# Attention and routed experts on one core: the third pair's keys on three engines, GpSimd's work in pieces, one transpose later, two weight splits later

## The chip, the cores and the metric

The kernel runs on one core of a Trainium2 chip. The metric is the device time of one execution in microseconds (us). A core has five engines that run side by side, each through its own instructions in order: TensorE (PE in the profile, with its weight loads as PEld), VectorE (DVE), ScalarE (ACT), GpSimd (POOL) and SyncE (SP), which here only issues DMAs. A profile line such as L223 is line 223 of the kernel before the change.

## The reference

Two parts follow each other. Attention works on 4 batches of 8 heads with 768 positions of 64 elements. Every query sees a window of 31 keys around itself and 24 summaries of blocks of 32 keys (the maximum of the keys, the mean of the values):

```python
k_sum = k.reshape(B, H, nb, block, D).max(axis=3)
v_sum = v.reshape(B, H, nb, block, D).mean(axis=3)
mask_l = np.abs(pos[:, None] - pos[None, :]) < window
scores_l = scale * np.matmul(q, k.transpose(0, 1, 3, 2))
scores_s = scale * np.einsum('bhsd,bhnd->bhsn', q, k_sum) + np.log(block)
a = softmax(concatenate([where(mask_l, scores_l, -1e9), scores_s], axis=-1))
x = a @ concatenate([v, v_sum], axis=2)
```

The rows x (4 x 768 rows of 512) then go through eight experts of two layers, one expert per row:

```python
for s in range(S):
    fresh_e = int(np.argmax(logits[b, s]))
    if s == 0 or local_gate[b, s] < 0.5: e = fresh_e
    else: e = prev_e if prev_e >= 0 else fresh_e
    prev_e = e
    h = np.maximum(x[b, s] @ w1[e], 0.0)
    out[b, s] = p[e] * (h @ w2[e])
```

A row may keep its predecessor's expert, so the choice is a scan along each batch.

## The kernel before

**Attention** handles two heads at once, a pair; there are 16 pairs, four per batch. A pair is cut into two groups of 384 queries, so 32 steps `G` run, with three more to drain. In step G, PE makes the scores of group G (`s_mm`: the mask by a small matmul, L255, then queries times keys, L261), transposes the probabilities of group G-2 (`t_stage`, L282, copied out by ScalarE at L283) and multiplies group G-3 with the values (`a_mm`, L293). VectorE takes the maximum of the scores (`s_exp`, L268), ScalarE the exponentials (L272), and VectorE divides (`a_norm`, L304 to L306).

**The keys and values of a pair are laid out ahead**, while the pair before is worked on. Keys lie transposed in `kp`; `windows` (L220 on GpSimd, L218 on ScalarE) copies 12 overlapping windows of 96 keys into `kb`, scaled; `reduce_k` (L201, VectorE) takes the maxima of 32 keys; `summaries` (L223) writes them, repeated 12 times, behind each window. The scores of the pair need all of that. For the block means of the values, `fold_v` (L210, GpSimd) adds the two halves of each block, `reduce_v` (L205, VectorE) sums what is left, `sum_v` transposes the sums on PE (L227) and copies them out on ScalarE (L229), and `spread_v` (L232, GpSimd) writes them 12 times into the value tile `vw`, which `a_mm` reads. Two buffers serve `kp`, `kb` and the transposed values `vt`, three serve queries and `vw`.

**Order.** The program writes every engine's order out by hand. The loads of all these tiles and the writes of finished rows to `x_dram` (L311) stand in one queue, SP's; each waits there for its buffer and for the end of an earlier DMA, and whatever is behind it waits too. The first pair's keys are laid out before the loop by three engines, half of the windows on ScalarE and half on GpSimd, with the summaries on VectorE. From the second pair on GpSimd does, in this order, windows and fold in a pair's first step, and summaries and the spread of the current pair in its second. In step 0 SP also loads three tables (`wg`, `c32`, `cb16`, 337 KB) that the routing of the first batch needs from step 10 on.

**Routing** of a batch begins when its four pairs are done. `x_tile` makes the logits (L460 to L491) in steps 10 to 15, 18 to 23 and 26 to 31; `route` (steps 15, 23 and 31 on) is a chain of some thirty small VectorE steps and five small PE steps that finds each row's expert. They are slipped between attention's instructions by a planner: three calls `small` per step, with 3, 2 and 4 places; each step of the chain names its engine, and a step on PE may only be taken `AGE` = 2 calls after the one before it, so that PE does not stand for it. L522 is the first of them, the transpose of `val`, which L519 finishes. After the second batch, `early` picks rows of the most frequent expert (L702 to L721, on PE L715) and gathers them (L984), so that expert work can start with the last batch still in routing.

**Weights of the first expert** are fetched in 8 chunks of 1024 columns (`WFETCH` gives the steps) and split into a high and a low part (`WSPLIT`, `WBY`): ScalarE casts (L970), then VectorE subtracts in one instruction (L973) or GpSimd in four (L978). Chunks 0 to 3 are split in steps 24, 25, 27 and 29, by GpSimd, VectorE, GpSimd, VectorE; the others behind attention, at the places in `WLAST`. Four staging tiles serve all eight, so chunk 6 waits for the split of chunk 2, chunk 7 for that of chunk 3.

**The experts** follow, three matmuls per product (high x high, high x low, low x high), L1039 to L1041 and L1012 to L1014, until the end.

Of the kernel before, what the change touches and what calls it, by code (L numbers as in the profile page):

```python
# [9 lines left out]
F32 = mybir.dt.float32  # L10
# [9 lines left out]
P = 128  # L20
NP = H // 2
NW = S // 64
# [17 lines left out]

WFETCH = (21, 21, 22, 22, 26, 27, 29, 31)
WSPLIT = (24, 25, 27, 29)
WBY = "GVGVVGVG"

# [11 lines left out]

AGE = 2
C_T, C_PE, C_WAIT, C_LONG, C_DVE, C_LAT, AHEAD = 0.65, 0.8, 0.3, 0.9, 0.1, 0.05, 1.5
# [4 lines left out]
class Kernel:  # L63
# [81 lines left out]
    def attention(self, tick, last):  # L145
        nc, tc, ident = self.nc, self.tc, self.ident
        with ExitStack() as ctx:
# [59 lines left out]
            def fold_v(n):  # L207
                f = wk.tile([P, S // 2], F32, name="vf", bufs=1)
                v = by32(vts.pop(n))
                nc.gpsimd.tensor_tensor(out=by32(f, 16), in0=v[:, :, 0:16], in1=v[:, :, 16:32], op=ALU.add)  # L210
                folded[n] = by32(f, 16)

            def windows(n, eng=nc.gpsimd, t0=0, t1=NW):

                src = kp[n % 2][:, 64 * t0:64 * t0 + 1]
                win = bass.AP(src.tensor, src.offset, [src.ap[0], (64, t1 - t0), (1, WL)])
                if eng is nc.scalar:
                    eng.activation(out=kb[n % 2][:, t0:t1, 0:WL], in_=win, func=AF.Copy, scale=0.125)  # L218
                else:
                    eng.tensor_scalar(out=kb[n % 2][:, t0:t1, 0:WL], in0=win, scalar1=0.125, scalar2=1.0, op0=ALU.mult, op1=ALU.mult)  # L220
# [10 lines left out]
            def spread_v(n):  # L231
                nc.gpsimd.tensor_copy(out=vw[n % 3][WL:W, :, :, 0:D],  # L232
                                      in_=vss.pop(n).rearrange("p (h d) -> p h d", h=2).unsqueeze(1).to_broadcast([NB, NW, 2, D]))

# [87 lines left out]
            for G in range(last_g + LA):  # L322
# [7 lines left out]
                tick(G, 2)  # L330
                if GP < G < last_g and G % GP == 0:
                    sum_v(G // GP, self.spare[:, 1, 0:P])
# [7 lines left out]
                if G < last_g:  # L340
                    s_exp(G)
                    self.small(3, True)
                if G == 0:
                    for t, src in consts:
                        nc.sync.dma_start(out=t, in_=src)
                tick(G, 0)
                if G < last_g:
                    self.small(2, True)
                n, g = divmod(G, GP)
                if g == 1 and 0 < n < len(pairs) - 1:  # L350
                    reduce_v(n + 1, folded.pop(n + 1))
# [3 lines left out]
                if G < last_g:  # L355
                    n, g = groups[G]
                    N = len(pairs)
                    if g == 0:
# [4 lines left out]
                        elif n + 1 < N:  # L363
                            windows(n + 1)
                            fold_v(n + 1)
                            reduce_k(n + 1)
                        if n + 2 < N:
                            load_v(n + 2)
                        if 1 < n + 1 < N:
                            load_w(n + 1)  # L370
                    else:
                        if n + 1 < N and n:
                            summaries(n + 1)
# [33 lines left out]
    def small(self, n, pe=False):  # L407
# [3 lines left out]
        while self.credit > 0:  # L411
            heads = [h for h in list(self.steps)[:2] if h[0] != "PE" or pe and h[2] <= self.calls - AGE]
            if not heads:
                return
            head = min(heads, key=lambda h: h[0] == "PE")
            if len(heads) == 2 and head is self.last:
# [4 lines left out]
    def step(self, head):  # L421
        kind = head[0]
        self.last = head
        if kind == "PE":
            head[3] = max(self.t, head[3]) + C_PE
# [17 lines left out]
    def flow(self, dt):  # L443

        self.t += dt
        while True:
            heads = [h for h in self.steps[:2]
                     if (h[3] <= self.t if h[0] in ("PE", "WAIT") else max(h[3], self.q) <= self.t + AHEAD)]
            if not heads:
# [44 lines left out]
    def route(self, b):  # L494
# [24 lines left out]
        v.tensor_copy(out=val[0:1, 0:1], in_=sv[0:1, 0:1])  # L519
        yield "PE"  # L520
        m = self.bank("t")
# [846 lines left out]
```

## Time and profile before

| | |
|---|---|
| three runs | 479.96, 480.21, 481.28 us, median 480.21 |
| the profiled execution | 479.85 us, of which span from first to last instruction 478.1 |
| PE busy | 441.2 us (92%) |
| VectorE, ScalarE, GpSimd busy | 256.9, 216.3, 214.8 us |
| mean granted clock of TensorE | 0.976 |
| GpSimd's windows, fold, summaries, spread | 1.15, 1.01, 0.43, 1.46 us each |

A row of the order of time reads: start, duration, engine, line, operation, tile written <- tiles read, shapes, how many instructions were merged, and in brackets how long the engine had stood idle and what ended that. The table of stretches gives, for each engine, busy time and number of instructions, then the granted clock as a share, the mean busy share of the 16 DMA engines and GB/s.

### The profile page before, as it was taken

The numbers are of one execution on the slowest core, as the hardware profiler recorded it, in microseconds if no ns is written. First come the engines' busy times: TensorE is split into PE (matmuls) and PEld (weight loads), VectorE is DVE, ScalarE is ACT, GpSimd is POOL, SyncE is SP. The second block draws the span as 40 slices with busy tenths as digits, with TensorE's granted clock in tenths as the row PEclk, the third lists the DMA queues.
The fourth block names the chain that finished last, engine by engine and source line by source line (L and its number), as shares of the span: only waits on it lengthen the run. The fifth ranks groups of instructions, "written<-read, shape, count | busy, mean of one in ns | idle before, by whom it ended". The sixth has DMA issues, their size and how long they took to land. (4 is left out here: it accounts for less than half of the span.)

```text
span 478.1 us, 11984 instructions
## 1 busy us (share of the span) xinstructions
PE 441.2 (92%) x4400; PEld 383.0 (80%) x4400; DVE 256.9 (54%) x602; ACT 216.3 (45%) x479; POOL 214.8 (45%) x227
## 2 busy tenths in 40 slices
PE   6699989969889999999999999999999999999990
PEld 6477768757778789897989898989789898978970
DVE  5477597888874777993122222272745227274520
ACT  4588778878655222721211111272664127266400
POOL 2387454566502330852020202075887207588820
PEclk9799999999799999999999999999999999999995
DMA  8899969997530191392020202038389403938840
GB/s 301 316 378 334 384 238 344 360 374 288 193 125 15 29 387 71 86 352 73 23 67 23 67 24 67 22 108 334 121 330 330 149 23 97 345 119 309 290 178 27
DMA packets 23623, 92.05 MB, mean 193 GB/s; under 512 B 2927, under 2 KB 3567, under 8 KB 19440
## 3 DMA queue, kind: packets, MB, share of 16 engines
q1 hardware_dynamic: 18752, 76.11, 43.1%
q0 software_dynamic: 4640, 14.68, 9.3%
q8 instruction: 41, 0.67, 0.6%
q14 instruction: 46, 0.38, 0.3%
q10 hardware_dynamic: 144, 0.20, 0.1%
HBM read 78.40 MB, written 13.11 MB: 191 GB/s over the span
## 5 line engine op out<-in xcount | busy, mean ns | idle before, releaser
L1041 PE MATMUL bs<-xT,l 128*128 128x256 f32 x384 | 108.9, 284 | 1.2 <-DVE l L973 1.2
L1039 PE MATMUL bs<-xT,h 128*128 128x256 f32 x384 | 109.9, 286 | 0.0
L1040 PE MATMUL bs<-xT,h 128*128 128x256 f32 x384 | 108.8, 283 | 0.4 <-DVE xT L990 0.4
L984 POOL DMA_INDIRECT xg<-x_dram,gidx x32 | 37.1, 1160 | 124.8 <-POOLq L1215 54.2
L1045 ACT ACTIVATE hT<-bs 128x512 fp32r<-128x512 f32 x48 | 28.7, 598 | 121.6 <-PE bs L1041 121.1
L1047 DVE SCALAR_TENSOR_TENSOR hT<-bs,hT 128x512 fp32r<-128x512 f32 x48 | 33.1, 690 | 90.7 <-ACT hT L1045 79.7
L1012 PE MATMUL ba<-h,hT 128*128 128x512 f32 x192 | 77.8, 405 | 0.4
L1014 PE MATMUL ba<-h,hT 128*128 128x512 f32 x192 | 75.1, 391 | 0.0
L1013 PE MATMUL ba<-l,hT 128*128 128x512 f32 x192 | 75.0, 391 | 0.0
L978 POOL TENSOR_TENSOR l<-stg,h 128x256 fp32r<-128x256 f32 x84 | 73.9, 915 | 2.3 <-ACT h L970 1.6
L1041 PEld LDWEIGHTS bs<-xT,l 128*128 128x128 f32 x384 | 73.5, 191 | 1.8 <-DVE l L973 1.8
L1040 PEld LDWEIGHTS bs<-xT,h 128*128 128x128 f32 x384 | 73.5, 192 | 1.3 <-DVE xT L990 0.8
L1039 PEld LDWEIGHTS bs<-xT,h 128*128 128x128 f32 x384 | 73.5, 191 | 0.7 <-issue 0.2
L970 ACT CAST h<-stg 128x1024 fp32r<-128x1024 f32 x56 | 57.2, 1053 | 11.9 <-PE ba L1014 10.9
L272 ACT ACTIVATE pr<-bs,nm 128x120 f32<-128x120 f32 x192 | 51.9, 371 | 14.0 <-DVE nm L268 10.5
L973 DVE TENSOR_TENSOR l<-stg,h 128x1024 fp32r<-128x1024 f32 x35 | 46.5, 1338 | 16.2 <-ACT h L970 13.1
L1025 POOL DMA_INDIRECT out_dram<-yo,sidx x26 | 28.2, 1085 | 46.7 <-DVE yo L1024 21.3
L1012 PEld LDWEIGHTS ba<-h,hT 128*128 128x128 f32 x192 | 36.1, 188 | 8.0 <-issue 0.5
L1014 PEld LDWEIGHTS ba<-h,hT 128*128 128x128 f32 x192 | 36.0, 188 | 7.9
L1013 PEld LDWEIGHTS ba<-l,hT 128*128 128x128 f32 x192 | 36.2, 189 | 6.2
L261 PE MATMUL bs<-kb,q 64*64 64x120 f32 x768 | 27.2, 276 | 8.3 <-POOL kb L223 7.6
L268 DVE TENSOR_REDUCE nm<-bs 128x6 f32<-128x720 f32 x32 | 28.7, 898 | 5.9 <-ACT l L481 2.7
(236 smaller groups left out, 661.7 us busy)
## 6 DMA issues: line engine op xcount, KB each, us to landing
stg<-in_w SPq DMA_DIRECT2D x32, 1024.0 KB, 6.8
vw<-in_vW SPq DMA_DIRECT2D x16, 780.0 KB, 6.9
kp<-in_kT SPq DMA_DIRECT2D x16, 384.0 KB, 5.4
q<-in_qT SPq DMA_DIRECT2D x16, 384.0 KB, 6.8
vt<-in_vT SPq DMA_DIRECT2D x16, 384.0 KB, 6.7
x_dram<-xs SPq DMA_DIRECT2D x8, 768.0 KB, 4.6
wst<-in_w SPq DMA_DIRECT2D x8, 512.0 KB, 7.1
xg<-x_dram,gidx POOLq DMA_INDIRECT x32, 3.8
```

The costliest lines, as they stand in the source:

```text
L272: nc.scalar.activation(out=pr[:, h, u, :], in_=sp[:, h, u, :], func=AF.Exp, bias=nm[:, h, u:u + 1], scale=1.0)
L970: self.nc.scalar.copy(out=hi, in_=src)
L973: eng.tensor_tensor(out=lo, in0=src, in1=hi.bitcast(F32), op=ALU.subtract)
L978: eng.tensor_tensor(out=lo[:, p], in0=src[:, p], in1=hi[:, p].bitcast(F32), op=ALU.subtract)
L984: self.nc.gpsimd.indirect_dma_start(out=t, out_offset=None, in_=rows, in_offset=bass.IndirectOffsetOnAxis(ap=self.gidx[:, i:i + 1], axis=0))
L1012: nc.tensor.matmul(out=ps, lhsT=ah, rhs=wh, start=first, stop=False)
L1013: nc.tensor.matmul(out=ps, lhsT=ah, rhs=wl, start=False, stop=False)
L1014: nc.tensor.matmul(out=ps, lhsT=al, rhs=wh, start=False, stop=last)
L1039: nc.tensor.matmul(out=ps[:, j], lhsT=wh, rhs=xh, start=(k == 0), stop=False)
L1040: nc.tensor.matmul(out=ps[:, j], lhsT=wh, rhs=xl, start=False, stop=False)
L1041: nc.tensor.matmul(out=ps[:, j], lhsT=wl, rhs=xh, start=False, stop=(k == KT - 1))
L1047: nc.vector.scalar_tensor_tensor(out=l, in0=ps, scalar=0.0, in1=h.bitcast(F32), op0=ALU.max, op1=ALU.subtract)
```

## The change

1. **Third pair's keys.** In step 2 the windows are halved between ScalarE and GpSimd and VectorE writes the summaries, as for the first pair. There is no fold for the third pair; VectorE sums its values whole, in step 4 instead of 3, and the transpose of the sums goes to step 5. The three tables are loaded in step 4 instead of 0. From the fourth pair on, the fold is written behind the maxima instead of ahead of them; these are different engines.
2. **GpSimd in pieces.** Windows go in pieces of at most 4 windows (three for a pair, two for a half), folds in two pieces, spreads in four.
3. **Routing's first transpose.** For the first two batches L522 is marked "PE late": it may be taken 3 calls after the step before it instead of 2.
4. **Splits.** Chunk 0 is split by VectorE and chunk 1 by GpSimd (swapped); chunk 2 stays with GpSimd and chunk 3 with VectorE, but they move from steps 27 and 29 to 30 and 31. Chunks 6 and 7 are fetched in steps 31 and 32 instead of 29 and 31.

```diff
-WFETCH = (21, 21, 22, 22, 26, 27, 29, 31)
-WSPLIT = (24, 25, 27, 29)
-WBY = "GVGVVGVG"
+WFETCH = (21, 21, 22, 22, 26, 27, 31, 32)
+WSPLIT = (24, 25, 30, 31)
+WBY = "VGGVVGVG"
...
-AGE = 2
+ON_PE = {"PE": 2, "PE late": 3}
...
             def fold_v(n):
...
+                for i in range(0, NB, NB // 2):
+                    p = slice(i, i + NB // 2)
+                    nc.gpsimd.tensor_tensor(out=f[:, p], in0=v[:, p, 0:16], in1=v[:, p, 16:32], op=ALU.add)
...
             def windows(n, eng=nc.gpsimd, t0=0, t1=NW):
+                if eng is nc.gpsimd and t1 - t0 > NW // 3:
+                    for t in range(t0, t1, NW // 3):
+                        windows(n, eng, t, min(t + NW // 3, t1))
+                    return
...
             def spread_v(n):
...
+                for t in range(0, NW, NW // 4):
+                    nc.gpsimd.tensor_copy(out=vw[n % 3][WL:W, t:t + NW // 4, :, 0:D], in_=vs.to_broadcast([NB, NW // 4, 2, D]))
...
-                if GP < G < last_g and G % GP == 0:
+                if 2 * GP < G < last_g and G % GP == 0 or G == 2 * GP + 1:
                     sum_v(G // GP, self.spare[:, 1, 0:P])
...
-                if G == 0:
-                    for t, src in consts:
-                        nc.sync.dma_start(out=t, in_=src)
...
-                if g == 1 and 0 < n < len(pairs) - 1:
+                if g == 1 and 1 < n < len(pairs) - 1:
                     reduce_v(n + 1, folded.pop(n + 1))
...
-                            windows(n + 1)
-                            fold_v(n + 1)
-                            reduce_k(n + 1)
+                            if n > 1:
+                                windows(n + 1)
+                                reduce_k(n + 1)
+                                fold_v(n + 1)
+                            else:
+                                windows(2, nc.scalar, 0, NW // 2)
+                                windows(2, nc.gpsimd, NW // 2, NW)
+                                reduce_k(2)
+                                summaries(2, nc.vector)
+                        if n == 2:
+                            reduce_v(2)
                         if n + 2 < N:
                             load_v(n + 2)
                         if 1 < n + 1 < N:
                             load_w(n + 1)
+                        if n == 2:
+                            for t, src in consts:
+                                nc.sync.dma_start(out=t, in_=src)
                     else:
-                        if n + 1 < N and n:
+                        if n + 1 < N and n > 1:
                             summaries(n + 1)
...
         yield "DVE"
         v.tensor_copy(out=val[0:1, 0:1], in_=sv[0:1, 0:1])
-        yield "PE"
+        yield "PE late" if b < 2 else "PE"
         m = self.bank("t")
         nc.tensor.transpose(out=m[0:NU, 0:P], in_=val, identity=self.ident)
```

More of the change, by code (lines that the diff above doesn't have):

```diff
@@ L207, in fold_v @@
             def fold_v(n):
-                f = wk.tile([P, S // 2], F32, name="vf", bufs=1)
+                f = by32(wk.tile([P, S // 2], F32, name="vf", bufs=1), 16)
                 v = by32(vts.pop(n))
-                nc.gpsimd.tensor_tensor(out=by32(f, 16), in0=v[:, :, 0:16], in1=v[:, :, 16:32], op=ALU.add)
-                folded[n] = by32(f, 16)
+                for i in range(0, NB, NB // 2):
+                    p = slice(i, i + NB // 2)
+                    nc.gpsimd.tensor_tensor(out=f[:, p], in0=v[:, p, 0:16], in1=v[:, p, 16:32], op=ALU.add)
+                folded[n] = f
             def windows(n, eng=nc.gpsimd, t0=0, t1=NW):
+                if eng is nc.gpsimd and t1 - t0 > NW // 3:
+                    for t in range(t0, t1, NW // 3):
+                        windows(n, eng, t, min(t + NW // 3, t1))
+                    return
                 src = kp[n % 2][:, 64 * t0:64 * t0 + 1]
@@ L231, in spread_v @@
             def spread_v(n):
-                nc.gpsimd.tensor_copy(out=vw[n % 3][WL:W, :, :, 0:D],
-                                      in_=vss.pop(n).rearrange("p (h d) -> p h d", h=2).unsqueeze(1).to_broadcast([NB, NW, 2, D]))
+                vs = vss.pop(n).rearrange("p (h d) -> p h d", h=2).unsqueeze(1)
+                for t in range(0, NW, NW // 4):
+                    nc.gpsimd.tensor_copy(out=vw[n % 3][WL:W, t:t + NW // 4, :, 0:D], in_=vs.to_broadcast([NB, NW // 4, 2, D]))
             folded = {}
@@ L411, in small @@
         while self.credit > 0:
-            heads = [h for h in list(self.steps)[:2] if h[0] != "PE" or pe and h[2] <= self.calls - AGE]
+            heads = [h for h in list(self.steps)[:2] if h[0] not in ON_PE or pe and h[2] <= self.calls - ON_PE[h[0]]]
             if not heads:
                 return
-            head = min(heads, key=lambda h: h[0] == "PE")
+            head = min(heads, key=lambda h: h[0] in ON_PE)
             if len(heads) == 2 and head is self.last:
@@ L423, in step @@
         self.last = head
-        if kind == "PE":
+        if kind in ON_PE:
             head[3] = max(self.t, head[3]) + C_PE
@@ L447, in flow @@
             heads = [h for h in self.steps[:2]
-                     if (h[3] <= self.t if h[0] in ("PE", "WAIT") else max(h[3], self.q) <= self.t + AHEAD)]
+                     if (h[3] <= self.t if h[0] in ON_PE or h[0] == "WAIT" else max(h[3], self.q) <= self.t + AHEAD)]
             if not heads:
```

## The prediction

> **What bounds the kernel now.** I read the page first, for the span and the slices; then the waits of TensorE (PE); then the order of time around each wait.
>
> ```profile
> span 478.1 us, 11984 instructions
> ...
> PE   6699989969889999999999999999999999999990
> ```
>
> A slice is 12 us. From the slice at 143 us on, when the experts have begun, PE is at nine tenths or more until the last: nothing of the change lies there, and time won earlier should move that stage forward whole. Before that lies attention, and there PE has holes. Its waits from 60 to 124 us (engine, line, what it waited for: us in total, times, longest):
>
> ```profile
> PE bt L522 <- DVE val L519: 2.7, 2, 1.4
> PE bs L261 <- POOL kb L223: 2.4, 1, 2.4
> PE bs L227 <- DVE va L205: 1.7, 2, 0.9
> PE bt L715 <- DVE ebt L711: 1.2, 1, 1.2
> ```
>
> These are 8.0 us, and each row meets a part of the change. A longer one stands at the start, in order of time:
>
> ```profile
> 13.14 1.56 ACT L272 ACTIVATE pr<-bs,nm 128x120 f32<-128x120 f32 x6
> 13.37 1.46 POOL L232 COPY vw<-vs 24x1536 f32<-24x1536 f32 x1 [3.69 <-ACT vs L229]
> 13.52 0.95 DVE L201 TENSOR_REDUCE ks<-kp 128x24 f32<-128x768 f32 x1 [1.65 <-DMA kp<-in_kT]
> ...
> 15.93 0.35 PE L255 MATMUL bs<-me 64*64 64x360 bf16 x4
> 19.45 1.00 POOL L210 TENSOR_TENSOR vf<-vt 128x384 f32<-128x384 f32 x1 [3.38 <-DMA vt<-in_vT]
> 20.42 0.43 POOL L223 TENSOR_SCALAR kb<-ks 128x288 f32<-128x288 f32 x1
> ...
> 20.90 1.11 PE L261 MATMUL bs<-kb,q 64*64 64x120 f32 x24 [4.63 <-POOL kb L223]
> ```
>
> The third pair's keys landed at 13.5, where the maximum of L201 starts; but on GpSimd (POOL) the key summaries of L223 stand behind the fold of L210, which waits until 19.45 for values. PE stands from 16.28 to 20.90 for an instruction whose own data was there.
>
> **Part 1, the start.** In the new order nothing of the third pair's keys stands behind the values. ScalarE (ACT) lays out its half after the exponentials, from 14.70. VectorE (DVE) ends the maximum at 14.47 and then writes the summaries, which take GpSimd 0.43. GpSimd is the last, and there the short pieces count. These are the sizes that the trace has (ns: shortest, median, longest):
>
> ```profile
> L220 POOL TENSOR_SCALAR kb<-kp x16: 675/1152/1741, 4.9 to 118.8; 128x1152 f32<-128x1152 f32 x15, 128x576 f32<-128x576 f32 x1
> L210 POOL TENSOR_TENSOR vf<-vt x14: 1002/1012/1020, 19.4 to 119.9; 128x384 f32<-128x384 f32 x14
> L978 POOL TENSOR_TENSOR l<-wst,h x16: 722/732/1513, 101.3 to 160.9; 128x256 fp32r<-128x256 f32 x16
> ```
>
> Windows of 1152 elements take 1.152 and of 576 take 0.675: 0.83 ns an element and 0.20 us an instruction (with two inputs 1.012 for 384 and 0.732 for 256: 2.2 ns and 0.17). An added piece costs about 0.17, since neighbours overlap by some 0.03 (L223 starts at 20.42, L210 ends at 20.45). No row shows the spread, L232, in another size; I take the same 0.17 for it, between 0 and its whole 1.46, which it would be if its time went by the instruction. Six pieces are added per pair, 1.0 on top of 1.15 + 1.01 + 0.43 + 1.46 = 4.05, so 5.05. The Trainium skill, GPSIMD Engine Reference, section 2.1, puts the dispatch of an instruction at "tens of cycles"; as an estimate, 50 cycles of its 1.2 GHz are 0.04 us, so by the page six pieces would cost 0.25, and the 0.2 that I take off below would go. No row here shows it so cheap.
>
> GpSimd then ends the spread at 13.37 + 1.46 + 0.5 = 15.3 and its half of the windows, in two pieces, at 15.3 + 0.85 = 16.2. PE's mask matmul ends at 16.28, so the scores start at 16.3 and not at 20.9: 4.6 won. What is late next? The pitch of the steps after the stall, and the stretches around it (us, busy time of PE, PEld, DVE, ACT, POOL, granted clock, DMA share, GB/s):
>
> ```profile
> 28.50 0.85 PE L261 MATMUL bs<-kb,q 64*64 64x120 f32 x24 [0.57 <-POOL kb L223]
> ...
> 33.72 0.79 PE L261 MATMUL bs<-kb,q 64*64 64x120 f32 x24
> 20.00:22.00 2.00, 1.10 (x25) 0.80 (x26) 1.45 (x5) 0.00 (x0) 0.85 (x2) 0.84 0.21 43
> 22.00:30.00 8.00, 7.43 (x126) 6.12 (x125) 5.62 (x12) 5.65 (x20) 5.44 (x5) 0.83 1.03 394
> 30.00:40.00 10.00, 10.00 (x233) 8.41 (x232) 9.02 (x20) 9.04 (x31) 7.78 (x8) 1.00 0.99 363
> ```
>
> Two steps take 33.72 - 28.50 = 5.2, so 2.6 each. Three things stand behind the new start.
>
> VectorE sums the third pair's values itself now, unfolded: the 768 elements of L201, so about its 0.95. Ahead of that, from 16.0 on, stand two normalisations, the second pair's sum, a maximum of scores and one of keys, which I estimate at the same 0.95 each, with a pause of 0.4 for PE's attention matmuls: it ends near 22.0. The transpose of that sum (L227, now a step later) is due on PE near 20.2. That is a new wait of 1.8, and the step's probability transposes are queued behind it.
>
> GpSimd does the second pair's spread from 19.2 to 21.2, then windows 1.5, fold 1.2 and summaries 0.43: 24.3. The fourth pair's scores, at 28.50 now, can start then: 4.2 won. The 1.8 is paid from the half clock after the stall, which the trace has at 0.83 over 8 us (1.4 lost). From there GpSimd needs 5.05 a pair where PE needs 5.2: it keeps up, barely, and I take 0.2 off.
>
> DMA is full from 22 to 40. Only the hole at 20 to 22 can be filled (2.0 x 0.79 = 1.6). On SP's queue the fourth pair's values, which wait for the fold's end at 20.45 now, will wait for VectorE's sum of the second pair's, near 18, with the next windows of values, keys and queries queued behind; the three tables that move from the first step to the third pair's first step (337 KB, 0.9 us at 363 GB/s) only change places. So data comes 1.6 earlier while 4.2 are wanted, and the rest must be slack between landing and use. There is some, since from 24 to 124 us two of thirteen folds waited for data:
>
> ```profile
> POOL vf L210 <- DMA vt<-in_vT: 6.3, 2, 3.8
> ```
>
> I take **4.0**, from 1.6 (only the hole filled) to 6.0 (4.6 and all of the 1.4).
>
> **Part 2, routing.** Small VectorE steps of routing are long beside GpSimd and short without it:
>
> ```profile
> 62.08 1.46 POOL L232 COPY vw<-vs 24x1536 f32<-24x1536 f32 x1
> ...
> 62.53 1.07 DVE L506 TENSOR_TENSOR eq<-l_all,mx 128x48 f32<-128x48 f32 x1
> ...
> 134.67 0.20 DVE L506 TENSOR_TENSOR eq<-l_all,mx 128x48 f32<-128x48 f32 x1
> ```
>
> L506 ends at 63.60, just behind L232 at 63.54: VectorE waited out the whole GpSimd instruction. With pieces of 0.5 to 0.6 it waits for the rest of one, 0.3 on average, instead of 0.87: 0.5 saved, and as much for its sister L508 beside the fold, so 1.0 per batch. The late transpose takes L522 behind the next step's scores and probability transposes, so PE no longer stands there 1.4 each time. Its two followers move a call as well, but by the planner's credits (3, 2 and 4 a step) the matmuls of L555 fall on the same call as before, so nothing later moves. With PE free, VectorE's own chain is the limit, so I count its 1.0 for each of two batches: **2.0**, from 0.4 to 4.4 (L522 and L227 whole).
>
> **Part 3, the first two splits.**
>
> ```profile
> 101.32 2.78 POOL L978 TENSOR_TENSOR l<-wst,h 128x256 fp32r<-128x256 f32 x4 [4.18 <-ACT h L970]
> ...
> 104.50 1.23 DVE L973 TENSOR_TENSOR l<-wst,h 128x1024 fp32r<-128x1024 f32 x1 [1.51 <-ACT h L970]
> ```
>
> GpSimd's split of step 24 holds the summaries, and with them PE for the 2.4 of the waits. With the two swapped that goes, but VectorE's split now stands in step 24, ahead of step 25's maximum: 1.23 and a wait for ScalarE's cast that I put at 0.8, about half of the 1.51. Against it that later split leaves VectorE, mostly beside other work; I count 0.4. GpSimd's split a step later is covered by its pause before the next windows. 2.4 - 2.0 + 0.4 = **0.8**, from -1.2 (that cover gone, 2.0 lost) to 2.4.
>
> **Part 4, the two moved splits.**
>
> ```profile
> 115.25 3.58 POOL L978 TENSOR_TENSOR l<-wst,h 128x256 fp32r<-128x256 f32 x4 [2.13 <-issue]
> ...
> 134.56 0.89 ACT L283 COPY pt<-bt 120x384 f32<-120x384 f32 x2
> L970 ACT CAST h<-wst 128x1024 fp32r<-128x1024 f32 x6 | 6.5, 1086 | 0.0
> 123.00:131.00 8.00, 7.86 (x112) 6.43 (x112) 5.87 (x21) 5.20 (x16) 3.37 (x3) 0.57 0.41 115
> ```
>
> At 115 GpSimd's work moves up by 3.6, so the VectorE steps ahead of L715 meet less of it: I take 0.8 of that wait's 1.2. The VectorE split that leaves step 29 frees VectorE where PE is the bound (7.86 of 8.0 at a clock of 0.57): nothing. In steps 30 and 31 a cast of 1.1 comes ahead of the copies at 134.56, on which PE's last attention matmuls wait, and on GpSimd the last spread comes behind a split of 2.8; the two delays run side by side: -1.1. The last two fetches go a step or two later on SP and are used well into the expert stage: nothing. Together **-0.3**, from -3.0 (split and spread in the open) to 1.2.
>
> Sum: 4.0 + 2.0 + 0.8 - 0.3 = **6.5**. The profiled execution took 479.85 (its span and 1.75 around it); the median of the three runs is 480.21, 0.36 more. 479.85 - 6.5 = 473.35, and with the 0.36 **473.7**.
>
> **Rivals.** *The clock too.* In the row of 123 to 131 PE runs at 0.57, behind a wait of only 1.2. If that wait shrinks and the clock stays full, PE's work there takes 7.86 x 0.57 = 4.5, and VectorE's 5.87 becomes the limit: 2 more, and with part 2 nearer its upper end 469 to 471.5. Against it, where such a stretch falls may differ from run to run. The Trainium skill, TensorE: Matmul & The Clock Gate, Part 1, ties half clock to a whole window of about 3.4 us without work; by that rule the 1.2 was not the cause, the stretch stays, and this rival falls.
>
> *The start given back.* The transfers set the pace from 22 to 40, and part 1 brings its 1.6; the sum is 4.1, and with parts 2 and 3 a little short 476 to 478. For it stands the DMA share of 0.99 to 1.03.
>
> *Not what it says.* VectorE gets no turn between GpSimd's pieces and waits for all of them; part 2 is 0 and the time 475.7. Against it, the four pieces from 115.25 took 3.58 and those from 101.32 took 2.78, so something did get between.
>
> *Slower.* GpSimd becomes the bound of the three pairs from 24 to 40, because a piece costs more than 0.17. With six pieces of p each the loss is 3 x (4.05 + 6p - 5.2); it eats the 6.5 and 1.4 more from p = 0.63 on, and with p = 0.8 it is 10.9 and the time 484.6. Only the spread could cost so much; the other rows say 0.2.
>
> **How the numbers follow.** About 0.3% (1.4 us) can be told from no change. Forecast 0.50 (472 to 476), clock 0.25, start given back 0.12, not what it says 0.04, slower 0.05, every part at its lower end and no change 0.04. Faster 0.91, within 0.04, slower 0.05. The range takes in the clock's case from 469.0 and the start given back up to 478.0.
>
> **What would show it.** Right: no wait of PE for L223 between 16 and 21, and full clock there; a wait of about 1.8 at L227 near 20 to 22; the fourth pair's scores near 24.3; L506 and L508 under 0.6; no wait at L522; an expert stage of unchanged length. Wrong: windows, fold or spread clearly over 1.5, 1.2 and 2.0 in their pieces; GpSimd without a pause and PE waiting on it from 24 to 40; waits for DMA there; or a last attention matmul that waits for the last spread by more than 1.

## The result and the profile after

The changed kernel takes 473.49 us (median of 4 runs, 471.6 to 473.81) where the kernel before took 480.08 in the same comparison: a ratio of 0.984, 95% interval 0.982 to 0.986, so 6.6 us less by the medians and 7.6 by the ratio. (Differences in us given with a ratio below are taken from it.) The ratios leave out two executions far above their fellows, one of 551 us of the kernel before and one of 844 us of the kernel with the second transpose late. The profiled execution took 473.66, with a span of 471.8 instead of 478.1. Its code has moved down: L261 is now L270 (scores), L223 L231 (summaries), L227 L235 (transpose of the value sums), L232 L242 (spread), L506 and L508 L523 and L525, L522 L539, L525 L542 (the scan `pm`), L528 L545 (the second routing transpose), L973 L990 and L978 L995 (splits on VectorE and GpSimd), L293 L302, L990 L1007, L1040 L1057.

PE's waits after the change (line, what it waited for: us in total, times, longest) answer to the first list of the prediction:

```profile
PE bt L545 <- DVE pm L542: 4.1, 2, 3.1
PE bs L235 <- DVE va L206: 2.6, 3, 1.9
...
PE ba L302 <- POOL vw L242: 2.4, 1, 2.4
...
PE bs L270 <- POOL kb L231: 0.4, 1, 0.4
...
PE bt L732 <- DVE ebt L728: 0.2, 1, 0.2
```

The three waits that the change was aimed at are gone or small: 7.6 for the summaries became 0.4, 2.7 at L522 became nothing, 1.2 for `ebt` became 0.2. Of the 2.6 for the summed values, 1.9 are the new wait near the start and 0.7 what is left of the 1.7 in routing. But 4.1 stands for the scan, which no row of before had, and 2.4 for the last spread. The start in order of time:

```profile
14.23 0.67 ACT L226 ACTIVATE kb<-kp 128x576 f32<-128x576 f32 x1
...
14.95 0.85 PE L270 MATMUL bs<-kb,q 64*64 64x120 f32 x24
15.01 0.82 POOL L228 TENSOR_SCALAR kb<-kp 128x384 f32<-128x384 f32 x2
...
21.19 0.28 PE L235 MATMUL bs<-ident,va 128*24 128x128 f32 x1 [1.92 <-DVE va L206]
...
23.74 1.41 PE L270 MATMUL bs<-kb,q 64*64 64x120 f32 x24
```

The scores of the third pair start at 14.95 instead of 20.90, beside GpSimd's half of the windows. They need not wait for it: a step's matmuls read six windows (`t = 2 * (NG * g + u) + c`, with `NG` = 3), and the pair's first step reads windows 0 to 5, which are ScalarE's half. The new wait at L235 is 1.92, and the fourth pair's scores start at 23.74. The two small VectorE steps of routing each run four times, for the first two batches beside GpSimd. In the first batch L508 stood beside the fold (L506, 1.07 us beside the spread, is in the prediction):

```profile
64.74 1.02 POOL L210 TENSOR_TENSOR vf<-vt 128x384 f32<-128x384 f32 x1
...
64.87 0.95 DVE L508 TENSOR_TENSOR eq<-eq,c 128x48 f32<-128x48 f32 x1
```

In the changed kernel:

```profile
58.16 1.84 POOL L242 COPY vw<-vs 24x384 f32<-24x384 f32 x4
...
58.61 0.55 DVE L523 TENSOR_TENSOR eq<-l_all,mx 128x48 f32<-128x48 f32 x1
...
60.09 1.46 POOL L228 TENSOR_SCALAR kb<-kp 128x384 f32<-128x384 f32 x3
...
60.43 0.22 DVE L525 TENSOR_TENSOR eq<-eq,c 128x48 f32<-128x48 f32 x1
```

L523 gets between the pieces of the spread and takes 0.55 instead of 1.07. L525 is short for another reason: it comes earlier, GpSimd's spread takes longer, and so it no longer stands beside the fold but beside the windows, where it takes 0.22, hardly more than the 0.21 of the third batch with GpSimd idle. The second batch has the same pairs of numbers within 0.01. GpSimd's order from 31 to 38 shows what its pieces take, and that it now waits for data three times:

```profile
31.97 1.46 POOL L228 TENSOR_SCALAR kb<-kp 128x384 f32<-128x384 f32 x3 [0.53 <-DMA kp<-in_kT]
33.88 1.15 POOL L213 TENSOR_TENSOR vf<-vt 128x192 f32<-128x192 f32 x2 [0.46 <-DMA vt<-in_vT]
...
36.16 1.84 POOL L242 COPY vw<-vs 24x384 f32<-24x384 f32 x4 [0.73 <-DMA vw<-in_vW]
```

Where the time was won is read off the start of the scores of some steps, of the first second-layer matmul, and of the two ends, each subtracted from that of before (51.72, 93.87, 113.09, 161.28, 465.70 and 478.07). "Again" is another execution of the same kernel on another chip; the other rows are the experiments below. Negative is later than before.

| kernel | step 13 | step 24 | step 28 | second layer | last matmul | span |
|---|---|---|---|---|---|---|
| changed | 3.9 | 4.7 | 4.3 | 5.2 | 5.3 | 6.3 |
| changed, again | 4.3 | 5.1 | 5.3 | 6.2 | 6.1 | 7.1 |
| part 1 alone | 4.0 | 3.8 | 3.2 | 4.0 | 4.7 | 4.6 |
| pieces alone | -2.2 | -1.2 | -0.8 | 1.0 | 1.2 | 1.7 |
| late transpose alone | -0.8 | -1.5 | -4.8 | -4.9 | -4.6 | -4.8 |
| splits alone | -0.2 | -0.2 | -3.3 | -2.1 | -2.4 | -2.6 |
| without late | 3.7 | 4.6 | 4.9 | 4.4 | 5.1 | 6.0 |
| without the swap | 3.9 | 4.7 | 4.9 | 4.3 | 4.1 | 4.8 |
| last two splits back | 3.6 | 4.4 | 5.1 | 6.9 | 6.8 | 7.8 |
| second transpose late too | 4.0 | 5.4 | 6.4 | 4.9 | 4.7 | 5.7 |
| splits in 25, 26, 27, 29 | 4.0 | 4.8 | 4.3 | 3.2 | 3.4 | 4.3 |
| the same, second transpose late too | 3.4 | 4.8 | 6.2 | 5.9 | 6.3 | 7.2 |
| finer pieces | 0.4 | 1.7 | 2.6 | 3.6 | 4.0 | 4.4 |

Each row is one execution; two executions of one kernel differ by up to 1 here. The one execution of before that they are subtracted from took 479.85, while the medians of before on the other chips are 481.1 to 481.4, so the ratios give more than the last column, by 0.1 to 3.1 us. A verdict on time needs the ratio of several runs, which each experiment gives against the kernel before on its own chip (481.1 to 481.4 there).

### The profile page after: what moved, and what is told of

Same layout as the page of the kernel before. It is cut to its first block, busy times and chain, and to the rows that moved or that the text cites. A ratio compares the mean times of both kernels' runs of the same rounds, so it can differ in the third digit from the quotient of the medians.

```text
span 471.8 us, 12078 instructions
## 1 busy us (share of the span) xinstructions
PE 440.5 (93%) x4400; PEld 383.6 (81%) x4400; DVE 254.9 (54%) x603; ACT 216.5 (46%) x480; POOL 225.2 (48%) x316
## 5 line engine op out<-in xcount | busy, mean ns | idle before, releaser
L1057 PE MATMUL bs<-xT,h 128*128 128x256 f32 x384 | 108.8, 283 | 0.5 <-DVE xT L1007 0.5
L995 POOL TENSOR_TENSOR l<-stg,h 128x256 fp32r<-128x256 f32 x84 | 74.6, 921 | 2.5 <-ACT h L987 1.6
L1057 PEld LDWEIGHTS bs<-xT,h 128*128 128x128 f32 x384 | 73.5, 192 | 1.4 <-DVE xT L1007 1.0
L990 DVE TENSOR_TENSOR l<-stg,h 128x1024 fp32r<-128x1024 f32 x35 | 47.4, 1364 | 16.3 <-ACT h L987 13.1
L242 POOL COPY vw<-vs 24x384 f32<-24x384 f32 x64 | 30.7, 521 | 8.7 <-ACT vs L237 6.1
L302 PE MATMUL ba<-vw,pt 120*64 120x65 f32 x768 | 31.5, 235 | 2.9 <-POOL vw L242 2.4
```

The source lines that it names most:

```text
L990: eng.tensor_tensor(out=lo, in0=src, in1=hi.bitcast(F32), op=ALU.subtract)
L995: eng.tensor_tensor(out=lo[:, p], in0=src[:, p], in1=hi[:, p].bitcast(F32), op=ALU.subtract)
L1057: nc.tensor.matmul(out=ps[:, j], lhsT=wh, rhs=xl, start=False, stop=False)
```

## The experiments

The theory after the result: the start is won by part 1, the pieces pay in routing, and the late transpose and the splits only exchange waits, because VectorE has little time to spare from step 24 on. The rivals: every part brings its own share, as the prediction summed it; or the data sets the pace and the start is partly given back.

**Part 1 alone** (label p1_start), on the kernel before:

```diff
+                                windows(2, nc.scalar, 0, NW // 2)
+                                windows(2, nc.gpsimd, NW // 2, NW)
+                                reduce_k(2)
+                                summaries(2, nc.vector)
...
+                        if n == 2:
+                            reduce_v(2)
```

with the later transpose of these sums, the later tables and the order of the fold that belong to it.

> The kernel before with part 1 alone: the third pair's keys on three engines, VectorE's own sum a step later, tables loaded later. No pieces, no late transpose, splits as before. By the prediction's steps the start is worth 4.0: the scores of the third pair near 15 to 16.3 instead of 20.90, a wait of PE for the summed values of 1.8 in step 5, the scores of step 13 about 3.9 earlier, all of it kept to the end: 476.1. If the transfers set the pace from 22 to 40, step 13 is only 1.6 earlier: 478.5. If the gain of the start needs the short pieces (the spread ahead of the windows ends later without them), the third pair's scores start 0.5 or more later than in the changed kernel and the fourth pair's too, and the gain at step 13 is under 3.

It takes 475.94; ratio 0.989 (0.987 to 0.990), 5.5 less. Step 13 is 4.0 earlier, as in the changed kernel with its pieces. So the start needs no pieces, and the transfers do not limit it to 1.6. The third pair's scores start at 15.71 here, 0.8 later than with pieces, since the attention matmuls ahead of them wait 0.68 for the whole spread. At step 13 nothing of that is left against the first execution of the changed kernel, and 0.3 against the second.

**The pieces alone** (p2_pieces):

```diff
+                if eng is nc.gpsimd and t1 - t0 > NW // 3:
...
+                for i in range(0, NB, NB // 2):
...
+                for t in range(0, NW, NW // 4):
```

> The kernel before with GpSimd's windows, fold and spread in three, two and four pieces, nothing else. By the prediction's steps: L506 and L508 under 0.6, so the wait at L522 (1.4 twice) shrinks by about 1.0 each time; GpSimd's 1.0 more per pair costs 0.1 to 0.2 at the start, where the fold waits for its values anyway: 1.8 won, 478.3. Rival: GpSimd was close to the bound, and 1.0 more per pair shows as new waits of PE for the summaries between 24 and 124: 481 or more. Rival: without the later transpose the saving in VectorE is not seen: 480.1, and L522 still waits 1.4.

478.4; ratio 0.993 (0.992 to 0.995), 3.4 less, more than the 1.8 expected. Yet at the start they cost 2.2. GpSimd and PE there:

```profile
26.31 1.46 POOL L226 TENSOR_SCALAR kb<-kp 128x384 f32<-128x384 f32 x3
27.73 1.15 POOL L212 TENSOR_TENSOR vf<-vt 128x192 f32<-128x192 f32 x2
28.85 0.43 POOL L229 TENSOR_SCALAR kb<-ks 128x288 f32<-128x288 f32 x1
```

```profile
29.33 0.85 PE L268 MATMUL bs<-kb,q 64*64 64x120 f32 x24 [1.96 <-POOL kb L229]
...
65.82 0.28 PE L233 MATMUL bs<-ident,va 128*24 128x128 f32 x1 [0.34 <-DVE va L205]
68.63 0.27 PE L529 MATMUL bt<-ident,val 128*6 128x128 f32 x1 [0.91 <-DVE val L526]
```

After the stall GpSimd has two pairs to lay out without a pause, and there its 0.8 more per pair lies in the open: the wait for the fourth pair's summaries is 1.96, not 0.57. The step behind that wait then takes 4.05 instead of 2.67 with PE busy throughout, at a mean clock of 0.62 instead of 1.00, so 1.4 of the 2.2 is lost to half clock in this execution. Part 1 removes that stall, and with it the place where pieces cost. In the first batch's routing the wait for the summed values is 0.34, not 0.86, and that for `val` 0.91, not 1.36: 1.0 in all, and steps 16 to 18 win 1.0.

**The late transpose alone** (p3_late):

```diff
-        yield "PE"
+        yield "PE late" if b < 2 else "PE"
         m = self.bank("t")
         nc.tensor.transpose(out=m[0:NU, 0:P], in_=val, identity=self.ident)
```

> The kernel before with the first routing transpose a call later for two batches, nothing else. By the prediction nothing later moves: the 2.7 of L522's waits go whole and nothing takes their place, 477.4. By the trace of the changed kernel the next routing transpose (L528) is the next that is late: it waits for pm 1 to 2 in each batch, and of the 2.7 between 0 and 0.8 is left: 479.3 to 480.1.

484.38; ratio 1.005 (1.004 to 1.007): 2.6 slower, under neither theory. PE's waits in the first batch:

```profile
69.26 0.92 PE L293 MATMUL ba<-vw,pt 120*64 120x65 f32 x24 [0.65 <-DVE xs L306]
71.14 0.19 PE L528 MATMUL bt<-ident,pm 6*128 6x6 f32 x1 [0.96 <-DVE pm L525]
78.33 0.17 PE L555 MATMUL bt<-sc,cb 128*128 128x8 bf16 x1 [0.56 <-DVE sc L551]
```

The wait of 1.36 at L522 is gone and three of 2.17 in all have come: 0.8 lost, and from step 13 to step 24 this profile loses 0.7. L555 itself stays at its place, behind the probability transposes of step 19, as the prediction said, but its input does not: three VectorE steps (L540 to L546) now come behind a maximum of keys instead of ahead of it, and the scan `sc` behind them (L551) starts just behind the start of a spread of 1.53 and takes 1.40 where it took 0.24 before. In the second batch the exchange is even up to step 26; then 3.5 more are lost in one step, in which the profile has half clock (104.7 to 114.9). Executions of this kernel at a higher mean clock were no faster, so what makes up the rest of the 2.6 stays open.

**The splits alone** (p4_splits):

```diff
+WFETCH = (21, 21, 22, 22, 26, 27, 31, 32)
+WSPLIT = (24, 25, 30, 31)
+WBY = "VGGVVGVG"
```

> The kernel before with the splits alone: the first two swapped between GpSimd and VectorE, the other two in steps 30 and 31, two fetches later. By the prediction 0.8 - 0.3: the 2.4 wait for the summaries in step 25 goes, VectorE is 2.0 later there, 479.6. By the trace of the changed kernel VectorE's split stands ahead of the routing scan (pm) of the second batch, which costs PE about 3 in step 25, so the swap alone loses 0.5 or more at step 27; the two moved splits win 1 to 2 in the steps 27 to 35, and the sum is 478.5 to 480. Rival: without the later transpose the scan is already through before the split, the 2.4 goes whole and the time is 478 or less.

481.53; ratio 0.999 (0.998 to 1.001): nothing. The 2.4 for the summaries is gone, and this has come:

```profile
PE bt L528 <- DVE pm L525: 3.3, 1, 3.3
```

Step 28 is 3.3 later than before, and 1.2 of it is won back behind it. Only 1.2 of the 3.1 lost from step 24 on is waiting; for the other 1.9 PE's own work takes longer, at half clock (the table of steps 24 to 28 below).

Four experiments undo or extend one thing in the changed kernel.

**Without the late transpose** (a_nolate): `"PE late": 2` in place of 3.

```diff
-ON_PE = {"PE": 2, "PE late": 3}
+ON_PE = {"PE": 2, "PE late": 2}
```

> The changed kernel with the first routing transpose taken after 2 calls again, not 3; all else as changed. By the prediction the late transpose takes PE off a wait, so without it PE waits 0.9 for val twice (val comes earlier beside the pieces) and the time is 474.5 to 475.3. By the runs so far the late transpose only hands its wait on to the next transpose (0.96 for pm in the first batch), so nothing changes in the first batch; in the second 3.3 for pm beside the split stay either way and 0.9 is added: 473.5 to 474.4. If the late transpose does harm of its own, as alone on the kernel before (2.6 slower), the time is 471 to 472.5.

472.77; ratio 0.982 (0.980 to 0.984), where the changed kernel has 0.984 on both of its chips (0.982 to 0.986 and 0.981 to 0.986): the same. In the first batch the 0.96 at L545 becomes 0.91 at L539 (steps 13 to 24 win 0.8 with it and 0.9 without). In the second batch PE waits 0.91 at L539 and 2.36 at L545 instead of 3.13 at L545 alone; that second wait was expected to stay at 3.1 or more. The late transpose is worth nothing here.

**Without the swap** (a_noswap):

```diff
-WBY = "VGGVVGVG"
+WBY = "GVGVVGVG"
```

> The changed kernel with chunk 0 split by GpSimd and chunk 1 by VectorE again; chunks 2 and 3 stay in steps 30 and 31. By the prediction's part 3 the swap is worth 0.8: 474.3, with the 2.4 wait for the summaries back in step 25. By the trace of the changed kernel the swap exchanged that wait for one of 3.1 for the scan pm behind VectorE's split: without it 3.1 shrinks to about 1.0 and 2.4 comes back, and the time is the same, 473 to 474. If the wait behind VectorE's split is the dearer one, because the maximum of the scores stands behind it too, the time is 472.5 or less.

475.29; ratio 0.988 (0.985 to 0.991), which overlaps the changed kernel's interval only at its edge: the same or up to 2 slower, above every time that was expected. Step 25 up to the next scores, first of the changed kernel, then of this one:

```profile
95.56 1.35 DVE L990 TENSOR_TENSOR l<-wst,h 128x1024 fp32r<-128x1024 f32 x1 [0.81 <-ACT h L987]
96.83 0.90 DVE L277 TENSOR_REDUCE nm<-bs 128x6 f32<-128x720 f32 x1
97.65 0.40 DVE L542 TENSOR_TENSOR_SCAN pm<-bt,zero 6x128 f32<-6x128 f32 x1
```

```profile
98.20 0.24 PE L545 MATMUL bt<-ident,pm 6*128 6x6 f32 x1 [3.13 <-DVE pm L542]
```

```profile
96.06 0.19 PE L545 MATMUL bt<-ident,pm 6*128 6x6 f32 x1 [0.96 <-ACT pt L292]
98.87 1.48 PE L270 MATMUL bs<-kb,q 64*64 64x120 f32 x24 [2.34 <-POOL kb L231]
```

VectorE's split waits 0.81 for ScalarE's cast and takes 1.35; the maximum and then the scan stand behind it, and PE stands 3.13 for the scan. Without the swap PE stands 0.96 and 2.34, together 3.30. In this step the swap exchanged one wait for another of the same size. Why the times without it are longer, if they are, these rows do not show.

**The last two splits back in steps 27 and 29** (a_oldplace):

```diff
-WFETCH = (21, 21, 22, 22, 26, 27, 31, 32)
-WSPLIT = (24, 25, 30, 31)
+WFETCH = (21, 21, 22, 22, 26, 27, 29, 31)
+WSPLIT = (24, 25, 27, 29)
```

> The changed kernel with chunks 2 and 3 split in steps 27 and 29 again, and chunks 6 and 7 fetched in steps 29 and 31; the swap stays. By the prediction's part 4 the move costs 0.3: 473.2 here. By the two traces the stretch from step 27 to the experts is 1 shorter in the changed kernel, so here it is 474.5: the wait of 1.2 for ebt (L732) comes back, the wait of 2.4 for the last spread goes.

472.37; ratio 0.984 (0.981 to 0.986): the same as the changed kernel. Its waits behind step 30, then the changed kernel's:

```profile
124.30 0.92 PE L302 MATMUL ba<-vw,pt 120*64 120x65 f32 x24 [1.06 <-DVE ex L682]
127.83 0.92 PE L302 MATMUL ba<-vw,pt 120*64 120x65 f32 x24 [1.81 <-DVE xs L315]
```

```profile
127.90 1.48 PE L302 MATMUL ba<-vw,pt 120*64 120x65 f32 x24 [2.38 <-POOL vw L242]
```

The 2.38 for the last spread becomes 1.06 and 1.81, together 2.87, ahead of attention's last matmuls. The second layer starts 1.7 earlier with the old places than in the first execution of the changed kernel and 0.7 earlier than in the second, but the times cannot tell them apart.

**The second routing transpose late too** (a_late2):

```diff
         v.tensor_tensor_scan(out=pm, data0=m[0:NU, 0:P], data1=self.zero[0:NU, 0:P], initial=0.0, op0=ALU.max, op1=ALU.max)
-        yield "PE"
+        yield "PE late" if b < 2 else "PE"
```

> The changed kernel with the second routing transpose (L545) late as well for the first two batches. If the waits of 1.0 and 3.1 for pm hold up only PE, both go and 3 to 4 are won: 469.5 to 470.5. If in the second batch VectorE itself is late behind its split (the maximum of step 25's scores stands behind it too), the wait moves to the next step that needs VectorE: 1 to 2 won, 471.5 to 472.5. If a late step only hands its wait on, as the first one did, nothing is won: 473.5, with the wait at L551 or L572.

475.05; ratio 0.988 (0.985 to 0.990): nothing won. Both waits of L545 go, and step 24 comes 0.6 and 0.3 earlier than in the two executions of the changed kernel. Then these come:

```profile
97.92 0.28 PE L235 MATMUL bs<-ident,va 128*24 128x128 f32 x1 [2.38 <-DVE va L206]
...
133.31 0.39 PE L1057 MATMUL bs<-xT,h 128*128 128x256 f32 x1 [2.63 <-DVE xT L1007]
```

The same VectorE, later by the same work, is waited for at another line, in step 26. Step 28 still comes 2.1 (1.2) earlier: PE is idle no less than in the changed kernel from step 24 on, but this execution has no half clock there. That is lost again where the experts begin: PE stands 2.63 for the low part of `xT`, which VectorE makes, instead of 0.5 (1.7).

**Splits in steps 25, 26, 27 and 29** (b_slots), and **the same with the second transpose late** (b_slots_late2), beside the changed kernel itself on the same chip (a_again):

```diff
-WFETCH = (21, 21, 22, 22, 26, 27, 31, 32)
-WSPLIT = (24, 25, 30, 31)
-WBY = "VGGVVGVG"
+WFETCH = (21, 21, 22, 22, 26, 27, 29, 31)
+WSPLIT = (25, 26, 27, 29)
+WBY = "GVGVVGVG"
```

> The changed kernel with the four splits elsewhere: chunk 0 by GpSimd in step 25 and chunk 2 by GpSimd in step 27, behind the spread, chunk 1 by VectorE in step 26, chunk 3 by VectorE in step 29; chunks 6 and 7 fetched in 29 and 31. If the waits of step 25 come from a split in step 24 (GpSimd's holds the summaries 2.4, VectorE's the scan 3.1), both are gone here: L545 waits about 1.0, L270 not at all, 2 to 3 better than with the swap in step 24; and with no VectorE split in step 31 the wait for xT at the first expert is under 0.6. 469.5 to 471 on a chip where the changed kernel takes 473.5. If VectorE is simply short of time from step 25 to 27, the split of step 26 moves the wait there and nothing is won.

> The same splits, and the second routing transpose late too. If a late step frees PE only where VectorE has time to spare, the 1.0 at L545 goes in both batches and 1 to 2 more are won: 468.5 to 470. If what was won in attention is lost where the experts begin, because VectorE's chain to the low part of xT sets that time, the first expert matmuls come earlier, L1057 waits 1.5 to 2.6 for xT, and the time is that of the kernel without it.

> The changed kernel itself, unaltered, timed again beside the three others of this call. If the difference to before is a property of the kernel and not of one chip, it is 7 to 8 us faster than the kernel before here too (ratio 0.983 to 0.986). Its profile tells which of the places differ from execution to execution with nothing changed: half clock by the first profile at 22, 97 and 128. If such a stretch is fixed by the wait ahead of it, the three stand in the same places again; if it depends on how the wait falls on the gate's own windows, they do not, while the waits themselves are the same to 0.1.

Ratios 0.985 (0.982 to 0.987) and 0.984 (0.981 to 0.987), the changed kernel 0.984 (0.981 to 0.986): no difference. In the first of them the wait of step 25 is down to 0.96 with none for the summaries, and the split that went to step 26 makes the next one:

```profile
102.74 1.36 DVE L990 TENSOR_TENSOR l<-wst,h 128x1024 fp32r<-128x1024 f32 x1 [1.78 <-ACT h L987]
...
105.74 0.19 PE L572 MATMUL bt<-sc,cb 128*128 128x8 bf16 x1 [2.70 <-DVE sc L568]
```

At the first expert L1057 waits 0.3 for `xT` in the first of them and 2.2 in the second, as their expectations have it.

From the start of step 24's scores to those of step 28, every kernel's profile gives (us):

| kernel | length | PE busy | PE idle | VectorE busy | granted clock |
|---|---|---|---|---|---|
| before | 19.2 | 13.9 | 5.3 | 16.9 | 1.00 |
| part 1 alone | 19.8 | 15.1 | 4.8 | 17.0 | 0.91 |
| pieces alone | 18.8 | 15.1 | 3.8 | 15.1 | 0.91 |
| late transpose alone | 22.5 | 17.6 | 4.9 | 16.8 | 0.77 |
| splits alone | 22.3 | 15.9 | 6.4 | 18.7 | 0.85 |
| changed | 19.6 | 15.9 | 3.7 | 15.3 | 0.83 |
| changed, again | 19.0 | 14.9 | 4.1 | 15.4 | 0.91 |
| without late | 18.9 | 15.0 | 3.9 | 16.0 | 0.91 |
| without the swap | 19.0 | 15.1 | 3.9 | 14.8 | 0.91 |
| last two splits back | 18.6 | 14.9 | 3.7 | 15.4 | 0.91 |
| second transpose late too | 18.2 | 14.0 | 4.2 | 15.0 | 1.00 |
| splits in 25, 26, 27, 29 | 19.8 | 14.9 | 4.8 | 15.8 | 0.88 |
| the same, second transpose late too | 17.9 | 14.0 | 3.9 | 14.5 | 1.00 |
| finer pieces | 18.3 | 14.9 | 3.4 | 14.7 | 0.91 |

The pieces alone take PE's idle time from 5.3 to 3.8. The late transpose and the splits, in whatever arrangement beside them, leave it at 3.7 to 4.8; only finer pieces bring it lower. PE's idle time goes with VectorE's busy time over the rows. What hides the gain is the clock: PE's work takes 1.0 to 3.7 longer in the eleven profiles with half clock in this stretch, and before has none there. Step 25, and the stretch ahead of the experts, in the changed kernel (us, busy time of PE, PEld, DVE, ACT, POOL, granted clock, DMA share, GB/s):

```profile
92.25:98.67 6.42, 3.09 (x65) 2.47 (x60) 5.50 (x12) 4.22 (x13) 4.25 (x7) 0.90 0.95 380
121.40:134.70 13.30, 10.36 (x165) 8.50 (x159) 11.31 (x45) 8.87 (x24) 5.46 (x9) 0.87 0.38 128
```

VectorE is busy 5.50 of 6.42 and 11.31 of 13.30, more than any other engine. That it sets the time there is argued from these rows; it also waits 0.81 for ScalarE's cast in the first stretch. No kernel with parts 1 and 2 alone was run, so what the late transpose and the splits are worth together beside them is known only from undoing one at a time. No arrangement tried was faster than the changed kernel by more than its interval.

**Finer pieces** (a_more): windows in 6, fold in 4, spread in 12.

```diff
-                if eng is nc.gpsimd and t1 - t0 > NW // 3:
+                if eng is nc.gpsimd and t1 - t0 > NW // 6:
...
-                for i in range(0, NB, NB // 2):
+                for i in range(0, NB, NB // 4):
...
-                for t in range(0, NW, NW // 4):
+                for t in range(0, NW, NW // 12):
```

> The changed kernel with GpSimd's pieces cut further: windows in 6, fold in 4, spread in 12 (22 instructions of these a pair instead of 9). At 0.13 to 0.17 for an added piece that is 1.7 to 2.2 more per pair, so GpSimd needs about 6.5 a pair where PE needs 5.2 from 24 to 40: PE waits for the summaries of three pairs, 3 to 6 lost there, and the small VectorE steps of routing are no shorter than 0.4 to 0.5: 476.5 to 479. If finer pieces pay through the shared port, L523 and L525 fall to 0.2 and the time is 473.5 or less.

476.96; ratio 0.991 (0.988 to 0.993): 3.2 of the gain lost, at the lower end of what was expected.

```profile
32.27 2.88 POOL L242 COPY vw<-vs 24x128 f32<-24x128 f32 x12
35.24 1.92 POOL L228 TENSOR_SCALAR kb<-kp 128x192 f32<-128x192 f32 x6
37.13 1.43 POOL L213 TENSOR_TENSOR vf<-vt 128x96 f32<-128x96 f32 x4
38.52 0.43 POOL L231 TENSOR_SCALAR kb<-ks 128x288 f32<-128x288 f32 x1
```

GpSimd runs without a pause from 32 to 42 and needs 6.66 a pair where PE needs 5.2; by that sum three pairs lose 4.4. Step 13 is 3.5 later than in the changed kernel. PE waits 1.11 and 1.06 for the summaries (25.23 and 39.01) where the changed kernel waits 0.39 once; 1.3 of the 3.5 is PE's own work in the step behind the first of these waits, 4.81 instead of 3.49, at a clock of 0.50 instead of 0.73. So the prediction's slower rival is brought about in part: its mechanism, GpSimd's time per pair against PE's, is seen, and half clock adds to it. The first batch's routing wins 1.3 instead of 0.8 (steps 13 to 24).

## Why the prediction was right, point by point

The forecast was 473.7 and the time is 473.49, with 6.5 less forecast and 6.6 measured by the medians (7.7 on the second chip). The mechanism of the largest term was right. In the rest of the sum errors cancel, and that it comes out within 0.1 is luck.

- **Part 1, 4.0: right in size and, in the main, by its own steps.** Step 13 is 3.9 and 4.3 earlier. The wait at L235 is 1.92 (1.8 was put), the fourth pair's scores start at 23.74 (24.3). One step was wrong: GpSimd's half is not the last thing that the third pair's first scores wait for, since they read ScalarE's half alone, and so they start 1.3 earlier than put. At the fourth pair's scores 4.8 and 5.3 are won, not 4.2, and more is given back than the 0.2 put. In the first execution half clock from 22.2 to 25.6 takes 0.8 in the next step; full clock there, which the prediction named as a sign, holds in the second only. GpSimd waits for three transfers between 31 and 37 and PE once for 0.39 behind it, and the gain at step 10 is 3.4 before it is 3.9 again at step 13.
- **The price of a piece, 0.17: nearly right.** Windows take 1.15, 1.46 and 1.92 in 1, 3 and 6 pieces, folds 1.01, 1.15 and 1.43 in 1, 2 and 4, spreads 1.46, 1.84 and 2.88 in 1, 4 and 12: 0.15, 0.14 and 0.13 for an added piece. The Trainium skill, GPSIMD Engine Reference, section 2.1, has tens of cycles for an instruction's dispatch, an estimated 0.04 us; the rows say three to four times that.
- **Routing, 1.0 for the first batch: right, in part by another way.** Steps 13 to 24 win 0.8, all at full clock, and the pieces alone win 1.0 there. L523 shrank as said, from 1.07 to 0.55. L525 shrank more than said, from 0.95 to 0.22, because it left the fold's side, not because it got between pieces. The Trainium skill, SBUF — State Buffer, section "Who interferes with whom", says that a VectorE instruction with two SBUF inputs contends with a GpSimd instruction that reads SBUF, and calls the port pair that they share an exclusive lock. L523's 1.07 beside a whole spread, 0.55 beside one in four pieces and 0.21 beside one in twelve agree; L525's 0.22 beside the windows, which read SBUF too, shows no such wait.
- **The late transpose: wrong.** The step that failed is "so nothing later moves". L555 keeps its place, as put, but L528 moves and VectorE's steps ahead of L555 come later, one of them beside a whole spread (1.40 instead of 0.24). Alone it costs 2.6; in the changed kernel it exchanges 0.91 at L539 for 0.96 at L545.
- **The first two splits, 0.8: too large.** The 2.4 for the summaries goes (2.34 in the pair of runs), and VectorE's split costs 2.17, from 0.96 to 3.13 at the scan behind the maximum, where 2.0 was put. Of the 0.4 set against it nothing is seen. What is left is 0.17; the times leave room for up to 2, of which no trace shows the place.
- **The second batch, 1.0: right in waits, lost in time.** With the pieces PE's idle time from step 24 to 28 falls by 1.5, in the changed kernel by 1.6 (1.2 in the other execution). But PE's own work takes 2.0 (1.0) longer at half clock, so the stretch wins -0.4 (0.2). The step that failed is that the sum counts waits at full clock; it has no term for half clock in this stretch, where the profile of before has none.
- **The moved splits, -0.3: of no size that the times show.** What the prediction named as a sign against it came true: attention's matmuls wait 2.38 for the last spread, so that term was mis-sized at 1.1. But the old places have 1.06 and 1.81 there instead.
- **Not in the sum:** from step 28 to the second layer 0.9 was won, in both executions of the changed kernel (47.3 instead of 48.2). The pieces alone win 1.8 there and part 1 alone 0.8, so it does not need the moved splits. PE's own work is 1.3 and 2.6 shorter there (clock 0.96 and 1.00, before 0.93) and its idle time 0.4 and 1.7 longer. The last 1.0 lies behind the last matmul: from its end to the span's end it takes 12.4 to 12.6 in the four profiles without pieces (before, part 1, late, splits) and 11.3 to 11.9 in the ten with them. Why is open.

Of the rivals, *start given back* did not come to pass (3.9 stands at step 13, though a part is lost at step 10), and *not what it says* is refuted by L523, which starts and ends inside one spread. *Slower* needed a piece of 0.63, and pieces took 0.13 to 0.15; even the finer pieces are faster than before. *The clock too* is the subject of the last section.

## What to carry to other kernels

Over a stretch, before and after an edit, add up all of an engine's idle time, not one wait, and set its own busy time and the granted clock beside it: a gain in waits can be hidden by work at half clock. Where another engine is busy nearly all the time (VectorE, 5.50 of 6.42 us), a removed wait came back at the next line that needed it in each arrangement tried here; what lowered PE's idle time were the pieces, with which VectorE was busy for 15.1 us instead of 16.9 from step 24 to 28. More instructions on an engine off the path cost their fixed price only where that engine has no slack; count its time per round against the bound's. A deferred step needs the same question as a removed wait: what is queued behind it, and who reads that.

## What the runs showed of the hardware

The half clock is not fixed by a wait. The changed kernel's two profiles have nearly the same waits (1.92 and 1.91 at L235, 3.13 and 3.13 at L545, 2.38 and 2.12 at L302). The first, in stretches:

```profile
18.80:22.20 3.40, 1.49 (x31) 1.08 (x25) 2.63 (x5) 1.35 (x6) 3.32 (x8) 1.00 0.98 383
22.20:25.60 3.40, 3.40 (x55) 2.91 (x54) 1.95 (x5) 2.18 (x9) 2.58 (x6) 0.50 1.01 337
...
93.90:97.30 3.40, 0.97 (x25) 0.81 (x24) 2.59 (x3) 2.39 (x6) 2.40 (x4) 1.00 1.04 420
97.40:104.00 6.60, 5.80 (x65) 5.30 (x66) 3.55 (x12) 5.28 (x16) 4.32 (x8) 0.50 0.70 228
124.60:128.00 3.40, 1.02 (x9) 0.64 (x11) 3.26 (x12) 2.52 (x9) 3.33 (x6) 1.00 0.00 0
128.10:131.40 3.30, 3.30 (x42) 2.84 (x41) 2.68 (x9) 2.35 (x5) 1.11 (x3) 0.50 0.58 176
```

The second:

```profile
19.70:23.10 3.40, 1.75 (x35) 1.51 (x35) 2.66 (x4) 1.30 (x5) 3.31 (x7) 1.00 1.01 390
22.20:25.60 3.40, 3.40 (x84) 2.93 (x83) 2.90 (x6) 3.26 (x11) 2.62 (x7) 1.00 1.01 342
...
98.30:101.70 3.40, 3.40 (x45) 3.08 (x39) 1.89 (x5) 2.91 (x9) 1.56 (x3) 0.50 0.61 211
...
128.00:131.40 3.40, 3.21 (x58) 2.64 (x58) 3.33 (x16) 2.37 (x6) 0.25 (x1) 1.00 0.60 194
```

Three stretches of half clock against one, not counting the span's last microseconds, which have it in both. Ahead of each in the first stand 3.4 us in which PE was busy for 1.0 to 1.5; in the second the same wait at L235 falls across two such windows, of 1.75 in the later one, and the clock stays. The Trainium skill, TensorE: Matmul & The Clock Gate, Part 1, says that the window is free-running and the effect varies from run to run: the two profiles agree. It also ties half clock to an idle window; here windows with PE busy for up to 1.49 of 3.4 were followed by it, and in the kernel before one of 2.17:

```profile
120.30:123.70 3.40, 2.17 (x46) 1.74 (x48) 3.33 (x10) 2.18 (x8) 2.48 (x3) 1.00 0.69 283
```

So PE's busy time in the window ahead, 1.75 without half clock behind it and 2.17 with, does not decide it alone. The prediction took that rule to keep the stretch at 123 to 131 in place; it is neither there nor gone, but comes and goes.

Over the whole kernel half clock is cheap. From step 28 to the second layer the first execution has PE busy for 42.6 us and idle for 4.7, the second, at full clock, 41.3 and 6.0: the same 47.3, since PE waits for others instead. The two spans are 471.8 and 471.0. Compared within each kernel, one us less of half clock goes with 0.15 us less span on average over the executions of all the kernels (worked out from mean clock and span of each; from -0.1 to 0.4 by kernel).
